# S4D convolution and 16-head attention on one core: set 0 of the seeds last and kept on chip, the first maxima's row ahead of the late stores, eleven products a job

## The chip, the cores and the metric

The kernel runs on one core of a Trainium2 chip. The time is the device's, in microseconds, of one execution; a kernel is judged by the median of several. An execution's profile gives the span from its first to its last instruction, and what each engine did in it: PE (TensorE: products; its weight loads are listed apart as PEld), DVE (VectorE), ACT (ScalarE), POOL (GpSimd) and SP, which here only issues DMA transfers. PE reads its operands from SBUF, the on-chip memory, and writes to PSUM, a second memory of eight banks, from which DVE and ACT evict results.

## The reference

Two independent halves are put side by side in the last axis (896 columns).

```python
# A: a diagonal state-space convolution; L = 2048, D = 448 channels, N = 256 states
dt = exp(log_dt);  A = -exp(log_A_real) + 1j*A_imag;  C = (C_real + 1j*C_imag) * dt[:, None]
K = 2 * einsum("dn,dnl->dl", C, exp((A*dt[:, None])[:, :, None] * arange(L))).real
a = irfft(rfft(u^T, 2L) * rfft(K, 2L))[:, :, :L]^T + u * D_skip
# B: full attention; S = 2048, 16 heads of 28 columns
q, k, v = split(x @ wqkv)
b = (softmax(q k^T * 28**-0.5) v) @ wo
out = concatenate([a, b], -1)
```

All is float32.

## The kernel before

**Seeds.** The convolution's kernel K is built for 56 blocks of eight channels. A block starts from its seeds: low powers of exp(A dt) (the `e` part, 256 columns), of the C-weighted ones (`g`), and factors (`zz`) with which POOL and DVE later double the powers up. Seeds are made in eight sets of seven blocks (`seeds(o)`, `BO = 7`). A set goes through stages: load the parameters into `nat`, scale them (ACT), transpose them on PE (`turn`, into the PSUM tile `pn`), sizes, sines and cosines (`tri`, ACT and DVE), then the tables: `e` into a tile taken from the ring of three `qhat` tiles, `g` and `zz` into an `sg` tile (two of them). POOL clears two columns of the `e` tile first (`places`, a memset). `put_e` and `put_g` store both to DRAM (`sd_d`).

**Projections.** In the same stage x (four chunks of 512 rows) is turned on PE and split into a high part `xh` and a rest `xl`, and the weights likewise, since a float32 product is made of three products in a shorter format: high by high, low by high, high by low. Of the 448 inner rows 112 are taken at a time (`CK`, `NCK`), so that a job, 512 columns of q or k for a group of four heads, or 128 rows of v, takes 4 x 3 = 12 products into one PSUM tile `pm`. There are 48 jobs. ACT and DVE split the result again into `hl` (for the last chunk's q a tile `xn`), and SP stores it to DRAM; q, k and v come back in the layout that attention wants (`qhat`, `khat`, `v`; `load_q`, `load_k`, `load_v`). `kdif` holds differences of k, from which the maxima are made with fewer reductions.

The code of this stage is written in slots, one stage of seeds against a share of the jobs. A scheduler then sets the order on each engine; from `nc.kept = KEPT["a"]` on, the program order is kept.

**Maxima.** Attention goes through 16 units: four groups of heads by four chunks of queries. Softmax needs, for each query, a bound on its scores; four products for each of 16 tiles of queries give it (`max_mm`, `max_pair`; ACT evicts one into `rl`, DVE adds and reduces). For the first unit this is a stage of its own. `max_end` turns the result and makes the row `mh` of it on DVE, and `max_put` sends that row by DMA into `qhat`, so that the score product subtracts it. The second unit's first three tiles (`LEAD = 3`, twelve products) come next; then the steps begin.

**Steps.** Each of 256 steps (16 units by 16 tiles of keys) has four score products `pss`, four exponentials `p` on ACT, eight products with v into `po`, four products `pm` for the maxima LEAD + 16 steps ahead, and between them slots for the convolution: powers of the seeds on POOL (`e_power`) and DVE (`g_powers`), blocks, transforms of u, spectra and outputs. `ORDER` sets the order in a step. Seeds are loaded as `sdb`, three blocks ahead. The next group's keys are loaded while the second unit of a group runs.

What the DMA queues do is set by program order too: SP issues one transfer after another, and a transfer whose wait isn't over holds the rest. In the profile nearly all instructions carry L75, the line of the recording helper; so groups are told apart by tiles.

Of the kernel before, what the change touches and what calls it, by code (L numbers as in the profile page):

```python
# [8 lines left out]
F32 = mybir.dt.float32  # L9
# [18 lines left out]
CK = 112  # L28
NCK = D // CK
# [12 lines left out]
SGB, XB, XL = 2, 5, 4  # L42
# [10 lines left out]
NO = 8  # L53
BO = NB // NO
# [36 lines left out]
def body(ctx, tc, a, out):  # L91
# [50 lines left out]

    kt_g, kd_g, q_u, m_u, mh_u, o_u, rl_u = {}, {}, {}, {}, {}, {}, {}
# [82 lines left out]
    with ExitStack() as st:  # L226
        sst, xst, wst = ExitStack(), ExitStack(), ExitStack()
        t_p = pool(sst, "t_p")
# [19 lines left out]
        def load_nat(o, queue=nc.sync):  # L248
            nats[o] = s_p.tile([PO, 4, 256], F32, name="nat", bufs=2)
# [5 lines left out]
        small = s_p.tile([128, BO, SDF - F_G], F32, name="sg", bufs=SGB)  # L255
# [6 lines left out]
        load_nat(0, nc.scalar)  # L262
# [34 lines left out]
        w_g = k0_t[:CK].rearrange("p g (i s k h e) -> p i s k g h e", i=2, s=2, k=NCK, h=HG)  # L297
        vh = y_p.tile([CK, NCK, D], F32R, name="vh")
        vl = y_p.tile([CK, NCK, D], F32R, name="vl")
        nc.gpsimd.memset(k0_t[:CK].rearrange("p g (n e) -> p (g n) e", e=32)[:, :, DH:].bitcast(F32), 0.0)  # L300
# [5 lines left out]
        for i in range(2):  # L306
            wn = t_p.tile([128, 3, LV, BO * 16], F32, name="tri", bufs=2).rearrange("p t k h -> p (t k h)")
            wn = wn[:CK, :2 * 3 * D].rearrange("p (k s d) -> p k s d", k=2, s=3)
# [22 lines left out]
        def seeds(o):  # L331
# [53 lines left out]
            def places():  # L385
                se = q_p.tile([128, HG, CQ], F32R, name="qhat", bufs=3).bitcast(F32).rearrange("p h q -> p (h q)")
                q["se"] = se = se[:, :BO * F_G].rearrange("p (b f) -> p b f", f=F_G)
                q["sg"] = sg = s_p.tile([128, BO, SDF - F_G], F32, name="sg", bufs=SGB)
                q["e8"] = se.rearrange("p b (c h e) -> p b c h e", c=2, e=8)
                q["g4"] = sg[:, :, :F_Z - F_G].rearrange("p b (c h e) -> p b c h e", c=2, e=4)  # L390
# [73 lines left out]
        def transposes(c):  # L464
            for k in range(NCK):
                pt = ps_t.tile([128, CQ], F32, name="pt")[:CK]
# [3 lines left out]
                xl[k] = x_p.tile([CK, CQ], F32R, name="xl", bufs=XL)  # L470
                nc.scalar.activation(xh[k], pt, AF.Copy)
                nc.vector.tensor_tensor(xl[k], pt, xh[k].bitcast(F32), ALU.subtract)

        def qk_proj(c, s, g):
            pp = w_tile()
            n = 0
            for k in range(NCK):
                for i, x_ in ((0, xh), (1, xh), (0, xl)):
                    nc.tensor.matmul(pp, w_g[:, i, s, k, g].rearrange("p h e -> p (h e)"), x_[k],
                                     start=n == 0, stop=n == 3 * NCK - 1)  # L480
# [28 lines left out]
        def v_proj(c, t):  # L509
# [3 lines left out]
            for k in range(NCK):  # L513
                for w_, x_ in ((vh, xh), (vl, xh), (vh, xl)):
                    nc.tensor.matmul(pp[:, :D], x_[k][:, ts], w_[:, k, :], start=n == 0, stop=n == 3 * NCK - 1)
# [17 lines left out]
        stages = [seeds(o) for o in range(NO)]  # L533
# [27 lines left out]
        for t in range(n_stage):  # L561
# [4 lines left out]
            if t + 1 == PW:  # L566
# [21 lines left out]
        max_end(0, ps_t.tile([128, CQ], F32, name="pt"))  # L588
        max_put(0, nc.scalar)
# [12 lines left out]
    k_pools = [k0_p, kq_p]  # L602
# [52 lines left out]
    def load_sd(b, queue=nc.sync):  # L655
        sds[b] = g_p.tile([128, SDF], F32, name="sdb", bufs=4)
        queue.dma_start(sds[b], sd_d[b // BO][b % BO])

    def k_seeds(b):

        if b not in es:
            es[b] = e = g_p.tile([128, 2, 16, N2], F32, name="e", bufs=2)
            nc.scalar.activation(e[:, :, :, :8], sds[b][:, :F_G].rearrange("p (c h e) -> p c h e", c=2, e=8), AF.Copy)
        else:
            g = g_p.tile([128, 2, 16, N1], F32, name="g", bufs=2)
            nc.scalar.activation(g[:, :, :, :4], sds[b][:, F_G:F_Z].rearrange("p (c h e) -> p c h e", c=2, e=4), AF.Copy)
            egs[b] = es.pop(b), g

    def k_start(b):
        zgs[b] = ps_g.tile([128, CQ], F32, name="zg")  # L670
        nc.scalar.activation(zgs[b][:, :Z_G], sds[b][:, SDF - Z_G:], AF.Copy)

    def e_power(b, i, q):

        t, m = egs[b][0], 8 << i
        zz = sds[b][:, F_Z:].rearrange("p (k f h) -> p k f h", k=6, f=3)
# [368 lines left out]
    for s in range(NS):  # L1045
# [20 lines left out]
        if kt % 4 == 1 and u % NQ == 1 and u // NQ + 1 < G:  # L1066
            load_k(u // NQ + 1, kt // 4, k_pools[(u // NQ + 1) % 2])
# [4 lines left out]
        for op in ORDER:  # L1072
# [96 lines left out]
```

## Time and profile before

| | |
|---|---|
| median of 3 runs | 1276.75 us (1276.06 to 1277.42) |
| the profiled execution | 1278.37 us, span 1276.6 us |
| mean granted TensorE clock | 0.985 |
| PE busy | 1223.9 us, 96% of the span |
| ACT, DVE, POOL busy | 967.5, 923.0, 846.2 us |
| DMA | 205.36 MB, 161 GB/s on average |
| chain that ended last | PE 75%, DVE 8%, POOL 6%, ACT 4%, DMA 3% |

A row of the timeline has the start, the duration, the engine, the operation, output tile <- input tiles, the shape, and in brackets how long the engine was idle ahead of it and what ended that. A group of instructions has its count, then busy time and the mean of one in ns, then idle time. SPq and ACTq are transfers being issued, not engines at work. A piece of the chain has start, duration and what it was.

### The profile page before, as it was taken

How to read it: one execution, taken by the hardware profiler on the slowest of the kernel's cores; microseconds unless marked ns; L12 is line 12 of the kernel's file. 1: busy time of each engine (PE TensorE's matmuls, PEld its weight loads, DVE VectorE, ACT ScalarE, POOL GpSimd, SP SyncE). 2: the span in 40 equal slices, each digit the busy share in tenths (PEclk: the TensorE clock that was granted, in tenths of full speed). 3: DMA queues.
4: the chain of work that ended last, by engine and by line, in shares of the span. 5: the costliest groups of instructions: out<-in, count | busy, mean ns of one | idle time of the engine just before them, and what ended most of it. 6: DMA issues, size and time to landing. Idle time of an engine off the chain costs nothing.

```text
span 1276.6 us, 33328 instructions
## 1 busy us (share of the span) xinstructions
PE 1223.9 (96%) x12641; PEld 699.3 (55%) x12641; DVE 923.0 (72%) x2106; ACT 967.5 (76%) x2162; POOL 846.2 (66%) x728
## 2 busy tenths in 40 slices
PE   7789887999999999999999999999999999999997
PEld 5667664555555555555555555555555545544433
DVE  6788866877777877877788888888897645645111
ACT  6878765788888888888878888888887666656452
POOL 2666750897788888878599999989995222324321
PEclk9889999899999999999999999999999999999999
DMA  7768699446564645375633133422324533657666
GB/s 216 244 223 288 233 304 346 113 93 186 160 149 113 168 119 168 113 235 167 176 94 104 49 88 97 154 81 71 88 54 156 179 131 135 204 170 228 198 170 167
DMA packets 200089, 205.36 MB, mean 161 GB/s; under 512 B 95992, under 2 KB 158520, under 8 KB 197880
## 3 DMA queue, kind: packets, MB, share of 16 engines
q1 hardware_dynamic: 199400, 202.63, 52.6%
q8 instruction: 100, 1.64, 0.5%
q10 hardware_dynamic: 528, 0.59, 0.2%
q14 instruction: 61, 0.50, 0.1%
HBM read 120.73 MB, written 82.18 MB: 159 GB/s over the span
## 4 chain that ended last, share of the span: by engine, by line
PE 75%; DVE 8%; POOL 6%; ACT 4%; issue 3%; DMA 3%; SPq 0%; ACTq 0%; POOLq 0%; DVEq 0%
PE pm L75 43%; PE pss L75 16%; PE po L75 16%; POOL e L75 2%; DVE tri L75 1%; ACT rl L75 1%; POOL qhat L75 1%; DVE mx L75 1%; DVE sg L75 1%; POOL eu L75 1%; ACT tri L75 1%; DVE px L75 1%; DVE qhat L75 1%; DVE hl L75 1%; DMA sd<-qhat 1%
## 5 line engine op out<-in xcount | busy, mean ns | idle before, releaser
L75 ACT ACTIVATE p<-pss 128x512 f32<-128x512 f32 x1024 | 561.0, 610 | 112.5 <-PE pss L75 107.2
L75 PE MATMUL pss<-qhat,khat 128*128 128x512 f32 x1024 | 403.2, 400 | 1.5 <-ACT p L75 1.4
L75 DVE TENSOR_REDUCE mx<-pm 128x1 f32<-128x512 f32 x480 | 308.6, 684 | 109.1 <-PE pm L75 107.2
L75 PE MATMUL pm<-khat,qhat 128*128 128x512 f32 x749 | 325.9, 438 | 6.4 <-ACT rl L75 4.2
L75 POOL TENSOR_TENSOR e<-e,sdb 128x256 f32<-128x256 f32 x168 | 201.8, 1201 | 110.6 <-ACT e L75 101.2
L75 PE MATMUL po<-p,v 128*32 128x512 f32 x2048 | 269.1, 594 | 0.0
L75 POOL TENSOR_TENSOR e<-e,eu 128x256 f32<-128x256 f32 x168 | 248.2, 1477 | 13.2
L75 PEld LDWEIGHTS pm<-khat,qhat 128*128 128x128 f32 x749 | 141.0, 189 | 201.9 <-ACT p L75 47.8
L75 DVE CUSTOM_DVE_ANT_0 rl<-pm,rl 128x512 f32<-128x512 f32 x259 | 178.3, 689 | 72.1 <-ACT rl L75 69.1
L75 PEld LDWEIGHTS pss<-qhat,khat 128*128 128x128 f32 x1024 | 190.6, 189 | 46.7 <-issue 10.8
L75 POOL TENSOR_TENSOR eu<-e,sdb 128x256 f32<-128x256 f32 x168 | 201.9, 1202 | 0.0
L75 POOL TENSOR_TENSOR p<-pr,pr 64x448 f32<-64x448 f32 x64 | 73.2, 1144 | 158.2 <-PE pm L75 132.8
L75 ACT ACTIVATE rl<-pm 128x512 f32<-128x512 f32 x259 | 156.6, 606 | 14.0 <-PE pm L75 8.4
L75 DVE TENSOR_TENSOR g<-g,zg 128x128 f32<-128x128 f32 x392 | 162.2, 414 | 3.4
L75 PE MATMUL pm<-kdif,qhat 128*128 128x512 f32 x249 | 100.5, 403 | 4.3 <-DVE xn L75 2.4
L75 PE MATMUL pm<-xh,khat 112*128 112x512 f32 x256 | 87.3, 425 | 4.9 <-DVE hl L75 1.8
L75 DVE TENSOR_TENSOR zg<-g,zg 128x128 f32<-128x128 f32 x224 | 88.0, 393 | 5.1
L75 PEld LDWEIGHTS pm<-e,g 128*32 128x32 f32 x3584 | 57.2, 109 | 43.4 <-issue 17.1
L75 DVE TENSOR_TENSOR pr<-pm,ub 128x448 f32<-128x448 f32 x64 | 37.0, 620 | 56.4 <-PE pm L75 42.0
L75 PE MATMUL pm<-e,g 128*32 128x64 f32 x3584 | 73.0, 222 | 1.8 <-POOL e L75 1.8
L75 ACT ACTIVATE y<-pm 128x448 f32<-128x448 f32 x48 | 26.5, 553 | 58.2 <-PE pm L75 36.2
L75 ACT ACTIVATE ub<-pm 128x224 f32<-128x224 f32 (+1 forms) x96 | 38.8, 449 | 39.7 <-PE pm L75 37.3
(134 smaller groups left out, 1461.8 us busy)
## 6 DMA issues: line engine op xcount, KB each, us to landing
sdb<-sd SPq DMA_DIRECT2D x55, 336.0 KB
qhat<-q SPq DMA_DIRECT2D x64, 256.0 KB
khat<-k SPq DMA_DIRECT2D x64, 256.0 KB
sd<-sg SPq DMA_DIRECT2D x8, 1456.0 KB
k<-hl SPq DMA_DIRECT2D x16, 512.0 KB
mw<-in_mw SPq DMA_DIRECT2D x16, 512.0 KB
sd<-qhat SPq DMA_DIRECT2D x8, 896.0 KB
yu_d<-ub SPq DMA_DIRECT2D x64, 112.0 KB
```

Source lines behind the costliest of these rows:

```text
L75: i = f(*args, **kw)
```

## The change

- The inner 448 rows are taken as 3 x 128 + 64 (`CK = 128`, `TL = 64`). The last 64 are laid twice into one tile of 128 partitions: x is loaded with its last 64 columns twice (a second, small transfer beside each x load), and after the turn the upper half of `xh` is overwritten with the rest, x minus its high part. The weights' last 64 rows are loaded twice as well. One product then gives high by high and high by low at once, a second the low weights by both: 2 products for this chunk, 3 x 3 + 2 = 11 a job.
- `nat` (two buffers), `sg` (two) and set 0's `e` now lie in one tile in the place of the second group's keys (a pool `k1_p` of its own, open from the start), instead of tiles of their own.
- Sets are made in the order 1 to 7, then 0. Set 0 isn't stored and loaded: its seven blocks are read where they were made. The second group's keys go into the same place, so they are loaded eight steps later (`KL = 8`).
- Of the set before (7), both stores are kept back (`kept`). Before, the two of the seventh set stood between the loads of v and q, and the last set's went in their turn, among the loads of keys.
- After the maxima, SP sends the row right behind the loads of q for two units and the first part of v; the other parts of v and the kept stores come after it. Before, ACT sent it, and then the first seeds.
- The second unit's lead stands right behind, in tiles of the whole stage's PSUM pools (`late_w`) and no longer in three of the next stage's.
- The first step has an order of its own (`ORDER_0`): scores first.

The diff, cut to its core:

```diff
-CK = 112
-NCK = D // CK
+CK = 128
+NCK = 4
+TL = D - 3 * CK
...
+ORDER_0 = ('s0', 's1', 's2', 'k', 's3', 'm0', 'm1', 'v', 'f', 'f', 'v', 'm2', 'm3', 'v')
+KL = 8
-SGB, XB, XL = 2, 5, 4
+XB, XL = 5, 3
+SETS = (1, 2, 3, 4, 5, 6, 7, 0)
...
+        k1_f = k1_p.tile([128, HG * L], F32, name="khat")
+        n_g, n_n = BO * (SDF - F_G), 4 * 256
+        sg_at = (0, HG * L - n_g)
+        sg_view = lambda i: k1_f[:, sg_at[i % 2]:sg_at[i % 2] + n_g].rearrange("p (b f) -> p b f", b=BO)
+        nat_view = lambda i: k1_f[:PO, n_g + i % 2 * n_n:n_g + (i % 2 + 1) * n_n].rearrange("p (a n) -> p a n", a=4)
+        se_view = k1_f[:, n_g:n_g + BO * F_G].rearrange("p (b f) -> p b f", b=BO)
...
-                xns[c, h] = y_p.tile([128, 2, CQ], F32, name="xn", bufs=3)[:, :, :D]
-                nc.sync.dma_start(xns[c, h], xs[:, 2 * h:2 * h + 2, :])
+                xns[c, h] = y_p.tile([128, 2, CQ], F32, name="xn", bufs=3)
+                for d, n, at in ((0, D, 0), (D - TL, TL, D)):
+                    nc.sync.dma_start(xns[c, h][:, :, at:at + n], xs[:, 2 * h:2 * h + 2, d:d + n])
...
-            nc.sync.dma_start(wns[k], wqkv[k * CK:(k + 1) * CK, :].rearrange("p (s d) -> p s d", s=3))
+            for p in range(1 if k < NCK - 1 else 2):
+                n = CK if k < NCK - 1 else TL
+                nc.sync.dma_start(wns[k][p * TL:p * TL + n], wqkv[k * CK:k * CK + n, :].rearrange("p (s d) -> p s d", s=3))
...
-                xl[k] = x_p.tile([CK, CQ], F32R, name="xl", bufs=XL)
                 nc.scalar.activation(xh[k], pt, AF.Copy)
-                nc.vector.tensor_tensor(xl[k], pt, xh[k].bitcast(F32), ALU.subtract)
+                if k < NCK - 1:
+                    xl[k] = x_p.tile([CK, CQ], F32R, name="xl", bufs=XL)
+                    nc.vector.tensor_tensor(xl[k], pt, xh[k].bitcast(F32), ALU.subtract)
+                else:
+                    nc.vector.tensor_tensor(xh[k][TL:], pt[TL:], xh[k][TL:].bitcast(F32), ALU.subtract)
...
-                for i, x_ in ((0, xh), (1, xh), (0, xl)):
+                for i, x_ in ((0, xh), (1, xh), (0, xl))[:3 if k < NCK - 1 else 2]:
...
-        kept_g, kept_e = (stages[NO - 2][i] for i in (-2, -1))
-        stages[NO - 2][-2:] = []
+        kept = stages[-2][-2:]
+        stages[-2][-2:] = stages[-1][-2:] = []
...
-                kept_e.pop()()
                 load_q(1)
-                for c in range(1, NQ):
-                    load_v(0, c)
-                kept_g.pop()()
...
         max_join(0, 2)
-        max_end(0, ps_t.tile([128, CQ], F32, name="pt"))
-        max_put(0, nc.scalar)
+        p_t, p_n, p_x = (lambda p=p, n=n: p.tile([128, CQ], F32, name=n) for p, n in ((ps_t, "pt"), (ps_n, "pn"), (ps_x, "px")))
+        max_end(0, p_t())
+        max_put(0)
+        for c in range(1, NQ):
+            load_v(0, c)
+        for f, in kept:
+            f()
+        late_w = [w_tile] * 3 + [p_t, p_n, p_n, p_x, p_t, p_n, p_n, p_x, p_t]
+        for i in range(LEAD):
+            for kc in range(4):
+                max_mm(1, i, kc, late_w[4 * i + kc])
         sst.close()
...
-    k_pools = [k0_p, kq_p]
+    k_pools = [k0_p, k1_p]
...
+    for b in range(BO):
+        sds[b] = se_view[:, b], sg_view(1)[:, b]
...
-    for b in range(3):
-        load_sd(b, nc.sync if b else nc.scalar)
-    for i in range(LEAD):
-        for kc in range(4):
-            max_mm(1, i, kc)
...
-        if kt % 4 == 1 and u % NQ == 1 and u // NQ + 1 < G:
-            load_k(u // NQ + 1, kt // 4, k_pools[(u // NQ + 1) % 2])
+        uk, kk = divmod(s - KL, NK)
+        if kk % 4 == 1 and uk >= 0 and uk % NQ == 1 and uk // NQ + 1 < G:
+            load_k(uk // NQ + 1, kk // 4, k_pools[(uk // NQ + 1) % 2])
...
-        for op in ORDER:
+        for op in ORDER if s else ORDER_0:
```

Three places in the built order. First PE behind the first unit's maxima, before; `pt<-ident,m` is the turn of the maxima, the products with kdif and khat are the second unit's lead, `pss` the first step's scores:

```order
L75 MATMUL pt<-ident,m_2286 16x128
L75 MATMUL pm_2326<-kdif_1585,qhat 128x512
L75 MATMUL pm_2330<-khat,qhat 128x512
L75 MATMUL pm_2333<-khat,qhat 128x512
L75 MATMUL pm_2336<-khat,qhat 128x512
L75 MATMUL pm_2339<-kdif_1585,qhat 128x512
L75 MATMUL pm_2343<-khat,qhat 128x512
```

and now:

```order
L79 MATMUL pt<-ident,m_2219 16x128
L79 MATMUL pm_2237<-kdif_1544,qhat 128x512
L79 MATMUL pm_2241<-khat,qhat 128x512
L79 MATMUL pm_2244<-khat,qhat 128x512
L79 MATMUL pt<-khat,qhat 128x512
L79 MATMUL pn<-kdif_1544,qhat 128x512
L79 MATMUL pn<-khat,qhat 128x512
L79 MATMUL px<-khat,qhat 128x512
L79 MATMUL pt<-khat,qhat 128x512
L79 MATMUL pn<-kdif_1544,qhat 128x512
```

The products are the same twelve; from the fourth on they are in other tiles than the three `pm`.

Second, SP's queue from the third part of the first group's keys on, before (`k_57` holds these keys in DRAM, `sd_87` and `sd_88` the last two sets of seeds, `q_1_66` the second unit's q, `v_94` to `v_97` v):

```order
L75 DMA khat<-k_57 32x2048 x4
L75 DMA sd_88<-sg 128x7x416
L75 DMA khat<-k_57 32x2048 x4
L75 DMA q_3_80<-xn 128x2x512
L75 DMA v<-v_94 128x512
L75 DMA sd_87<-qhat 128x7x256
L75 DMA v<-v_95 128x512
L75 DMA v<-v_96 128x512
L75 DMA v<-v_97 128x512
L75 DMA qhat<-q_1_66 32x4x512 x4
L75 DMA sd_87<-sg 128x7x416
L75 DMA sd_88<-qhat 128x7x256
```

and now:

```order
L79 DMA khat<-k_57 32x2048 x8
L79 DMA q_3_80<-xn 128x2x512
L79 DMA v<-v_94 128x512
L79 DMA qhat<-q_1_66 32x4x512 x4
L79 DMA qhat<-mh 1x16x128 x2
L79 DMA v<-v_95 128x512
L79 DMA v<-v_96 128x512
L79 DMA v<-v_97 128x512
L79 DMA sd_88<-khat 128x7x416
L79 DMA sd_88<-qhat 128x7x256
```

No store of seeds stands among the loads of keys any more, and the row `mh` has come over from ACT's queue.

Third, POOL at the second fill of a seed tile in a place that was used before, before (`qhat_706` and `qhat_927` are the second and third set's `e` tiles, `qhat_1324` the fifth's):

```order
L75 TENSOR_TENSOR qhat_706<-qhat_706,x_e_834 128x7x16x3
L75 MEMSET qhat_1324 128x7x16 x2
L75 TENSOR_TENSOR gz_872<-tri_721 128x2x112
L75 TENSOR_TENSOR qhat_927<-tri_721 128x7x16 x2
L75 TENSOR_TENSOR dhl_758<-kb_757,dhl_758 128x256
```

and now (`qhat_1082` is the fourth set's, `qhat_1293` the fifth's):

```order
L79 TENSOR_TENSOR dhl_955<-kb_954,dhl_955 128x256
L79 MEMSET qhat_1293 128x7x16 x2
L79 TENSOR_TENSOR tri_923<-tri_923 128x224
L79 TENSOR_TENSOR qhat_1082<-tri_923 128x7x16 x3
L79 TENSOR_TENSOR qhat_1082<-qhat_1082 128x7x16x3
```

The fill has moved from the end of the second set's work to the middle of the fourth's.

More of the change, by code (lines that the diff above doesn't have):

```diff
@@ L248, in load_nat @@
         def load_nat(o, queue=nc.sync):
-            nats[o] = s_p.tile([PO, 4, 256], F32, name="nat", bufs=2)
+            nats[o] = nat_view(SETS.index(o))
             for i, n in enumerate(("A_log_A_real", "A_A_imag", "A_C_real", "A_C_imag")):
@@ L465, in transposes @@
             for k in range(NCK):
[L466 removed]
+                pt = ps_t.tile([128, CQ], F32, name="pt")
                 for t in range(4):
@@ L532, in body @@
             work += jobs
-        stages = [seeds(o) for o in range(NO)]
+        stages = [seeds(o) for o in SETS]
         n_stage = SP * (NO - 1) + len(stages[0]) - SH
         slots = [[] for _ in range(n_stage)]
-        kept_g, kept_e = (stages[NO - 2][i] for i in (-2, -1))
-        stages[NO - 2][-2:] = []
+        kept = stages[-2][-2:]
+        stages[-2][-2:] = stages[-1][-2:] = []
         for o in range(NO):
@@ L653, in body, with load_sd @@
     sds, egs = {}, {}
-    def load_sd(b, queue=nc.sync):
-        sds[b] = g_p.tile([128, SDF], F32, name="sdb", bufs=4)
-        queue.dma_start(sds[b], sd_d[b // BO][b % BO])
+    def load_sd(b):
+        if b >= BO:
+            t = g_p.tile([128, SDF], F32, name="sdb", bufs=4)
+            sds[b] = t[:, :F_G], t[:, F_G:]
+            nc.sync.dma_start(t, sd_d[b // BO][b % BO])
+    for b in range(BO):
+        sds[b] = se_view[:, b], sg_view(1)[:, b]
     def k_seeds(b):
```

36 lines of the change are left out of this document (21 added, 15 removed).

## The prediction

> **What bounds the kernel now.** I read the five stages first (a table of windows cut at the places the chain and the timeline showed), because the change touches only what comes ahead of the attention steps. The columns are busy time per engine (instructions), the granted TensorE clock, the DMA share and GB/s.
>
> ```profile
> core 0: us, PE busy (x) PEld busy (x) DVE busy (x) ACT busy (x) POOL busy (x), PEclk, DMA share, GB/s
> 0.00:186.77 186.77, 160.65 (x706) 126.62 (x706) 145.89 (x288) 142.74 (x347) 108.68 (x149) 0.94 0.76 248
> 186.77:218.70 31.93, 24.75 (x81) 14.24 (x80) 23.06 (x68) 21.23 (x39) 1.88 (x2) 0.95 0.96 347
> 218.70:228.65 9.95, 7.13 (x15) 3.62 (x15) 5.70 (x14) 2.30 (x5) 1.08 (x2) 0.56 0.90 293
> 228.65:1236.00 1007.35, 997.98 (x11471) 541.65 (x11469) 741.48 (x1720) 786.25 (x1743) 726.71 (x574) 1.00 0.47 136
> 1236.00:1276.60 40.60, 33.43 (x374) 13.16 (x372) 6.90 (x18) 15.03 (x28) 7.84 (x4) 0.98 0.68 188
> ```
>
> From 228.65, where the first score product starts, PE is busy 997.98 of 1007.35 us: that stage is PE's own work, and the built order of PE, DVE and ACT after the first steps is the same in both kernels, apart from the tiles that ACT copies seeds from. So the result is decided by when the first score product starts. Ahead of it lie three stages: projections with seeds (186.77 us; PE 86% busy, DVE 78%, ACT 76%, no one engine full), the first unit's maxima (31.93), and the seam (9.95), in which nobody is busy and PE's clock is 0.56.
>
> For the first stage I read the chain of waits from 20 to 192 us: its shares, and its longest stretch of PE.
>
> ```profile
> by line: PE pm L75 12.3%; DVE tri L75 10.2%; issue 9.5%; POOL qhat L75 8.1%; DVE sg L75 7.0%; ACT tri L75 5.8%; DVE px L75 5.4%; DVE qhat L75 5.4%; DVE hl L75 5.0%; DMA sd<-qhat 4.8%; POOL x_e L75 3.3%; SPq L75 2.2%; DVE xl L75 2.2%; DMA kd
> 168.29 10.25 PE pm L75 x36
> ```
>
> The seeds (tri, sg, px, qhat) hold most of the chain, PE's products 12.3% of it, mainly at its end. That is the reason not to credit every product saved.
>
> **The change, part by part.**
>
> *Eleven products a job.* In the timeline three products follow in 0.70 us (184.43 to 185.13), 0.233 us each; in the groups of the first stage the xl products, of which a quarter goes, number 128 and 64.
>
> ```profile
> 184.43 0.40 PE L75 MATMUL pm<-xl,khat 112*128 112x512 f32 x1
> 184.67 0.62 PE L75 MATMUL pm<-xh,khat 112*128 112x512 f32 x2
> 185.13 0.40 PE L75 MATMUL pm<-xl,khat 112*128 112x512 f32 x1
> L75 PE MATMUL pm<-xl,khat 112*128 112x512 f32 x128 | 53.1, 423 | 0.1
> L75 PE MATMUL pm<-vh,xl 112*128 112x448 f32 x64 | 24.4, 388 | 0.0
> ```
>
> So 32 x 0.233 + 16 x 0.204 (448 of 512 columns) = 10.7 us of PE go. The last eight jobs are a pure PE stretch: 8 x 0.233 = 1.9 us, the lower bound; 10.7 is the upper. PE is the busiest engine but only an eighth of the chain, so I take a quarter of the other 8.8, in all -4.0. The DVE subtraction for the stacked chunk has as many columns as before and costs the same.
>
> *Dearer loads at the start.* The weights grow from 448 to 512 rows, and each of the two first x loads gets a 64 KB twin.
>
> ```profile
> tri<-in_B_wqkv SPq DMA_DIRECT2D x4, 588.0 KB
> 10.00:15.00 5.00, 4.38 (x14) 3.24 (x12) 3.62 (x7) 4.08 (x8) 1.37 (x2) 1.00 1.04 215
> 15.00:20.00 5.00, 5.00 (x22) 3.77 (x21) 2.33 (x10) 3.62 (x8) 2.23 (x2) 1.00 0.97 249
> ```
>
> 64/448 of 4 x 588 KB is 336 KB, with the twins 464 KB; at 215 to 249 GB/s, DMA being full there, 2.0 us. PE is at work in 15 to 20, and three jobs share the wait; between 0 and +2.0 I take +1.0. The six later twins are issued a chunk ahead of use, behind other products: 0. [...]
>
> *Fills of seed tiles.* POOL clears the tile of the set three ahead, and waits until that tile's earlier store has landed; what is queued behind it on POOL is the current set's work, and DVE waits for that.
>
> ```profile
> 67.05 2.10 POOL L75 TENSOR_TENSOR qhat<-qhat,x_e 128x336 f32<-128x336 f32 x1
> 69.18 4.11 DMA sd<-qhat
> 73.40 0.56 POOL L75 MEMSET qhat<- 128x112 f32 x2 [4.25 <-DMA sd<-qhat]
> 75.00:80.00 5.00, 3.88 (x22) 2.58 (x20) 1.89 (x5) 3.56 (x8) 3.35 (x7) 1.00 0.55 194
> ```
>
> The wait is on the chain (4.11 us), and DVE idles 3.1 us right after. In the built order this fill moves some fifteen POOL rows back, behind the whole third set, so that wait is over before it is reached. Bounds -4.25 and 0 (ACT's sines come next and could hold the set as long); I take -2.5, near DVE's idle time. The fill before it moves three rows only and I leave its wait. With set 0 last, one tile fewer is filled and one pair of stores goes: 7 x 128 x 672 x 4 B = 2.4 MB less traffic, hidden either way until the maxima.
>
> *The maxima.* The loads of khat now stand ahead of all late stores. The only break in this stage is here:
>
> ```profile
> 210.54 0.69 DVE L75 CUSTOM_DVE_ANT_0 rl<-pm,rl 128x512 f32<-128x512 f32 x1 [0.34 <-ACT rl L75]
> 211.30 0.50 PE L75 MATMUL pm<-kdif,qhat 128*128 128x512 f32 x1 [1.16 <-DVE mx L75]
> 212.18 0.69 DVE L75 CUSTOM_DVE_ANT_0 rl<-pm,rl 128x512 f32<-128x512 f32 x1 [0.94 <-PE pm L75]
> ```
>
> PE waits for a PSUM tile, not for the load: two kdif products stand one behind the other. They do so in the new order too, so 0.
>
> *The seam.* DVE finishes the row of maxima (mh) at 219.62; call this T.
>
> ```profile
> 219.34 0.28 DVE L75 SCALAR_TENSOR_TENSOR mh<-pt,mh 16x128 fp32r<-16x128 f32 x1
> 219.38 2.01 ACTq L75 DMA_DIRECT2D qhat<-mh  x2
> 221.43 0.60 ACTq L75 DMA_DIRECT2D sdb<-sd  x1
> 222.07 0.60 ACT L75 ACTIVATE rl<-pm 128x512 f32<-128x512 f32 x1 [4.46 <-issue]
> 222.70 0.69 DVE L75 CUSTOM_DVE_ANT_0 rl<-pm,rl 128x512 f32<-128x512 f32 x1 [3.09 <-ACT rl L75]
> 222.72 0.79 PE L75 MATMUL pm<-khat,qhat 128*128 128x512 f32 x1 [2.80 <-ACT rl L75]
> 224.40 0.81 SPq L75 DMA_DIRECT2D sdb<-sd  x2
> 227.92 1.28 DVE L75 TENSOR_REDUCE mx<-pm 128x1 f32<-128x512 f32 x2
> 228.65 0.63 PE L75 MATMUL pss<-qhat,khat 128*128 128x512 f32 x1
> 220.00:225.00 5.00, 2.28 (x4) 1.20 (x5) 1.90 (x4) 1.19 (x2) 0.00 (x0) 0.50 0.86 286
> ```
>
> ACT issues three transfers before it may evict the lead's first product: 2.6 us in which DVE and PE stand, PE with three tiles full. After that the lead crawls through three tiles at half clock, and the first score product comes at T + 9.0, with DVE's last lead reduction ending at 229.20, T + 9.6. Now the transfer is SP's, ACT's first eviction can end at T + 0.4, and DVE's three rounds (0.62 + 1.28 = 1.9 each) end at T + 6.1: 3.5 us earlier. The twelve lead products go round all eight PSUM banks; the last of them waits for DVE's fifth operation, T + 3.6, and the score follows at T + 3.9: 5.1 us earlier, if the row is there. SP's first wait behind the row ended at 224.40, T + 4.8 at most, with more stores ahead of it than now. So between -3.5 (DVE sets the early steps) and -5.1 I take -4.3. The v loads and set 7's stores stand behind the row on SP; v's first part is ahead of it, the others are wanted four steps apart. Seeds of blocks 0 to 6 need no load, so POOL starts early; in the steps POOL is 72% busy and gains nothing.
>
> *In the steps.* Khat of the next group is loaded eight steps later and waits for POOL's last reading of block 6; the maxima that want it are eight steps or more further, and DMA is 47% busy: 0.
>
> Sum: -4.0 + 1.0 - 2.5 - 4.3 = -9.8. The profiled run took 1278.37 us, so 1268.6 by its own time; it was 1.6 above the median of 1276.75, so I forecast 1267.0.
>
> **The rivals.**
>
> The front isn't shortened: the seeds' chain on DVE, POOL and ACT hides products and fill alike. For it speaks PE's 12.3%; against it the PE stretch at the end. Then only the start's +1.0 and the seam's -4.3: 1273.5.
>
> The front is PE's after all (86% busy): 10.7 and 4.25 in full, 1276.75 - 10.7 - 4.25 + 1.0 - 4.3 = 1258.5.
>
> The row doesn't travel under the lead, so that the change doesn't do what it says: SP is late for it, or it lands behind v loads, and the first score stays at T + 9. Against it: fewer stores are ahead. 1267.0 + 4.3 = 1271.3.
>
> Slower: the new order puts three nat loads of the fourth set behind two v stores on SP, where one stood.
>
> ```profile
> 45.12 0.62 SPq L75 DMA_DIRECT2D v<-vst  x1
> 45.79 0.84 SPq L75 DMA_DIRECT2D nat<-in_A_A_imag  x1
> 53.30 0.57 SPq L75 DMA_DIRECT2D v<-vst  x1
> 54.77 0.70 PE L75 MATMUL pn<-ident,nat 56*128 56x56 f32 x8 [2.76 <-ACT nat L75]
> 60.00:65.00 5.00, 4.17 (x12) 3.49 (x13) 5.00 (x12) 3.02 (x7) 3.65 (x4) 0.50 0.98 306
> ```
>
> Were they as late as the second store is here, 7.5 us, PE's in-order turn (which waits for them already) would move as far, and PE would run at 0.50 for three more such windows, 2.5 us each: +15.0 - 9.8 = +5.2, 1282.0. It decides once that delay and its half clock cost more than 9.8. Against it: the second store was late here because a seed store stood ahead of it, which now stands behind. [...]
>
> **How the numbers follow.** Forecast 0.47 (its own range 1263 to 1271: the seam's 3.5 to 5.1, the fill's 0 to 4.25, products 1.9 to 6), front not shortened 0.20, front PE's 0.12, row late 0.09, slower 0.07, mixed 0.05. The range goes from 1257.5, the PE rival, to 1276.0, past the first and third rival. A change under 0.2% (2.5 us) can't be told from none here; only a mix of a late row and an unshortened front (1277.8) falls there: same 0.05, slower 0.07, faster 0.88.
>
> **What would show it.** Right: the first score product near 219; no ACT issue between mh and the lead's first eviction; PE's clock at 1.00 through most of the lead; the second fill of a seed tile without a wait; 48 fewer products. Wrong: a first score product later than T + 6; the last projection product not before 184; new waits of PE for nat or of the score product for mh; a stage of steps longer than 1007 us, which I hold fixed and on which, with its size, the whole forecast hangs.

## The result, and the profile after

| | before | after |
|---|---|---|
| median of 20 runs, taken together | 1278.18 us | 1280.78 us |
| lowest and highest | 1276.06, 1280.87 | 1278.45, 1283.60 |
| profiled execution, span | 1278.37, 1276.6 us | 1279.05, 1277.3 us |
| products on PE | 12641 | 12593 |

The ratio is 1.0021 (95% interval 1.0014 to 1.0027): slower by 2.6 us, where 1267.0 was forecast. (The forecast started from the median of three runs, 1276.75, which lay 1.4 us under the median of twenty; what it forecast for the change is -9.8.) The two profiled executions differ by 0.68 us only, so the places below come from traces and the verdicts from medians. The front is everything up to the last projection product.

The five stages of the changed kernel, cut at the same events as the prediction's table (columns as there; first `kdif` product, turn of the maxima, first score, 1236, end):

```profile
core 0: us, PE busy (x) PEld busy (x) DVE busy (x) ACT busy (x) POOL busy (x), PEclk, DMA share, GB/s
0.00:187.91 187.91, 150.80 (x657) 118.31 (x658) 146.91 (x289) 142.35 (x349) 109.56 (x150) 0.93 0.75 248
187.91:219.80 31.89, 25.12 (x82) 14.14 (x80) 22.10 (x66) 20.82 (x37) 0.00 (x0) 0.95 0.66 244
219.80:224.90 5.10, 4.99 (x13) 2.98 (x14) 4.29 (x11) 2.29 (x5) 0.87 (x2) 0.67 0.32 100
224.90:1236.00 1011.10, 999.22 (x11467) 541.43 (x11468) 742.38 (x1723) 786.39 (x1743) 726.38 (x573) 1.00 0.46 137
1236.00:1277.30 41.30, 34.12 (x382) 13.46 (x374) 6.90 (x18) 15.03 (x28) 8.40 (x4) 0.99 0.68 190
```

In these two executions the first stage didn't shrink by 5.5 us (-4.0 + 1.0 - 2.5), it grew by 1.14 (187.91 against 186.77), although PE is busy 9.85 us less in it. The maxima are as long as before (31.89, 31.93). The seam is 5.10 instead of 9.95. So the first score product does start earlier, at 224.90 instead of 228.65. But the gain doesn't last. From T (mh ready: 219.62 before, 220.70 after) to the first score, and from there to the fourth step's first product with v, from which on both kernels keep one rhythm, it is before:

```profile
219.62:228.65 9.03, 6.23 (x13) 3.07 (x11) 5.15 (x12) 2.30 (x5) 1.08 (x2) 0.52 0.88 281
228.65:242.82 14.17, 14.17 (x100) 7.78 (x102) 12.15 (x29) 12.07 (x26) 13.62 (x13) 0.95 0.37 114
```

and after:

```profile
220.70:224.90 4.20, 4.09 (x11) 2.32 (x10) 3.73 (x9) 2.13 (x5) 0.87 (x2) 0.59 0.39 121
224.90:243.44 18.54, 15.95 (x101) 7.89 (x103) 13.59 (x32) 12.26 (x26) 16.02 (x15) 0.91 0.70 228
```

The lead is 4.83 us shorter, the first four steps are 4.37 longer; 0.46 is left. The timeline of those steps in the changed kernel shows the new waits:

```profile
225.33 1.58 ACT L79 ACTIVATE p<-pss 128x512 f32<-128x512 f32 x3 [1.18 <-PE pss L79]
...
227.47 0.62 ACT L79 ACTIVATE rl<-pm 128x512 f32<-128x512 f32 x1
228.12 0.69 DVE L79 CUSTOM_DVE_ANT_0 rl<-pm,rl 128x512 f32<-128x512 f32 x1 [1.44 <-ACT rl L79]
228.14 0.50 PE L79 MATMUL pm<-khat,qhat 128*128 128x512 f32 x1 [0.97 <-ACT rl L79]
...
230.78 0.50 PE L79 MATMUL pm<-khat,qhat 128*128 128x512 f32 x1 [1.17 <-DVE mx L79]
231.45 1.77 PE L79 MATMUL po<-p,v 128*32 128x512 f32 x8
```

With the four scores ahead, ACT makes all four `p` (three, then the copy `zg`, then one) before it evicts the first maxima tile at 227.47. DVE stands 1.44 us for it, PE then stands for ACT and for DVE, and its eight products with v take 1.77 us (1.10 in the kernel before): the granted clock is 0.56 in them.

In the front, two things stand out. POOL's waits at fills of seed tiles aren't gone:

```profile
58.93 0.50 POOL L79 MEMSET qhat<- 128x112 f32 x2 [1.20 <-DMA sd<-qhat]
98.23 0.52 POOL L79 MEMSET qhat<- 128x112 f32 x2 [2.35 <-DMA sd<-qhat]
114.91 0.57 POOL L79 MEMSET qhat<- 128x112 f32 x2 [6.96 <-DMA sd<-qhat]
```

That is 10.5 us in three waits, where 6.2 in two stood before. The second row is the fill that waited 4.25 us at 73.40. It comes 25 us later now and still waits 2.35, for the store of the second set's `e`; the third row's fill waited for nothing before. POOL's last product for that `e` ends at 66.77 here and at 69.15 before, but SP sent its store at 69.18 before (first fence) and sends it at 92.77 now (second):

```profile
69.18 0.37 SPq L75 DMA_DIRECT2D sd<-qhat  x1
```

```profile
91.84 0.36 SPq L79 DMA_DIRECT2D kd<-dhl  x1
92.30 0.42 SPq L79 DMA_DIRECT2D q<-hl  x1
92.77 0.48 SPq L79 DMA_DIRECT2D sd<-qhat  x1
```

The store stands behind others on SP, among them that of `kd`, for which SP stood 9.0 us until POOL had made `dhl`. And PE, with fewer products, waits for evictions more (for those of `hl` and `vst` 11.4 us in the first 188 us, 7.9 before):

```profile
125.51 0.94 PE L79 MATMUL pm<-xh,khat 128*128 128x512 f32 x2 [2.32 <-DVE hl L79]
```

### The profile page after: what moved, and what is told of

The parts are those of the page before. It is cut to its first block, busy times and chain, and to the rows that moved or that the text cites. A ratio compares the mean times of both kernels' runs of the same rounds, so it can differ in the third digit from the quotient of the medians.

```text
span 1277.3 us, 33236 instructions
## 1 busy us (share of the span) xinstructions
PE 1214.3 (95%) x12593; PEld 690.3 (54%) x12593; DVE 922.6 (72%) x2106; ACT 966.9 (76%) x2162; POOL 845.2 (66%) x728
## 2 busy tenths in 40 slices
DMA packets 199511, 201.39 MB, mean 158 GB/s; under 512 B 98040, under 2 KB 158776, under 8 KB 197304
## 4 chain that ended last, share of the span: by engine, by line
PE 77%; DVE 9%; ACT 5%; POOL 3%; DMA 3%; issue 2%; SPq 1%; ACTq 0%; POOLq 0%; DVEq 0%
PE pm L79 43%; PE pss L79 17%; PE po L79 17%; DVE tri L79 2%; DVE mx L79 1%; ACT tri L79 1%; DVE khat L79 1%; ACT rl L79 1%; SPq L79 1%; ACT p L79 1%; POOL qhat L79 1%; DMA khat<-k 1%; DVE px L79 1%; POOL p L79 1%; DVE hl L79 1%
## 5 line engine op out<-in xcount | busy, mean ns | idle before, releaser
L79 DVE TENSOR_REDUCE mx<-pm 128x1 f32<-128x512 f32 x475 | 305.2, 683 | 111.5 <-PE pm L79 109.5
L79 PE MATMUL pm<-khat,qhat 128*128 128x512 f32 x742 | 321.6, 436 | 5.6 <-DVE mx L79 3.1
L79 POOL TENSOR_TENSOR e<-e,sdb 128x256 f32<-128x256 f32 x147 | 176.6, 1201 | 64.6 <-ACT e L79 56.5
L79 PEld LDWEIGHTS pss<-qhat,khat 128*128 128x128 f32 x1024 | 190.7, 189 | 46.6 <-issue 10.8
L79 POOL TENSOR_TENSOR eu<-e,sdb 128x256 f32<-128x256 f32 x147 | 176.8, 1202 | 0.0
L79 PE MATMUL pm<-xh,khat 128*128 128x512 f32 x256 | 83.1, 418 | 10.1 <-DVE hl L79 6.5
```

What stands on the lines that cost most here:

```text
L79: i = f(*args, **kw)
```

## The experiments

Each time is a median, each ratio is to the kernel before, run beside it on the same chip, with its 95% interval. The kernel before stood between 1278.08 and 1278.28 throughout.

### The first step's order

`own_order`, on the changed kernel:

```diff
-        for op in ORDER if s else ORDER_0:
+        for op in ORDER:
```

> The changed kernel, with the usual step order in the first attention step too (maxima and scores in turn) instead of the order with four scores ahead. Theory A (the lead's gain is given back because four scores stand ahead of the first step's maxima: ACT copies four p tiles before it evicts the first maxima tile, DVE idles 1.44 us, PE then waits for DVE and its clock falls to half): the first two steps shrink by 1.5 to 4 us and the median comes to 1277 to 1279.5. Theory B (what PE, ACT and DVE have to do in the lead and the first steps is conserved, the order doesn't matter): within 0.7 us of the changed kernel's 1280.8.

Measured: 1277.74, ratio 0.9999 (0.9990 to 1.0008), so 3.0 us under the changed kernel. Theory A holds. In its trace T is 223.32 (its front ended later, see the last section), and the way from there to the fourth step is

```profile
223.32:227.60 4.28, 3.56 (x12) 1.93 (x11) 3.74 (x9) 2.20 (x5) 1.22 (x2) 1.00 0.43 126
227.60:242.21 14.61, 14.24 (x101) 6.89 (x103) 13.24 (x32) 12.07 (x26) 14.11 (x12) 1.00 0.88 287
```

The lead is as short as in the changed kernel, and the four steps take 14.61 us instead of 18.54: 18.89 in all against 23.20 before, 4.3 us less. That is the seam's whole forecast. Other traces below agree on the first step's order: with four scores ahead the four steps take 18.54 us in `after_as12` and 17.05 in `p12`, with the usual order 14.59 in `own_as12` and 15.70 in `best11`.

### The seam alone

`seam_own`, on the kernel before; nothing else of the change:

```diff
-                kept_e.pop()()
                 load_q(1)
-                for c in range(1, NQ):
-                    load_v(0, c)
-                kept_g.pop()()
...
-        max_put(0, nc.scalar)
+        max_put(0)
+        for c in range(1, NQ):
+            load_v(0, c)
+        for f, in (kept_g, kept_e):
+            f()
+        ...the lead in late_w, as in the change
```

> The kernel before with the seam alone: the row of maxima on SP's queue, the other v parts and the two kept stores behind it, the second unit's lead in all eight banks while it travels; twelve products, the seed order, and the usual step order as before. Theory A (the seam's gain is real where the first step keeps its order): 3.5 to 5 us faster than the kernel before (ratio 0.9961 to 0.9973). Theory B (work of the lead and the first steps is conserved): within 1 us (ratio 0.999 to 1.001).

Measured: 1279.99, ratio 1.0017 (1.0006 to 1.0027): neither. The lead was short (4.32 us), and then

```profile
226.75 0.42 ACT L75 ACTIVATE e<-sdb 128x256 f32<-128x256 f32 x1 [6.09 <-DMA sdb<-sd]
...
227.91 0.80 PE L75 MATMUL pm<-khat,qhat 128*128 128x512 f32 x1 [3.61 <-ACT rl L75]
```

ACT's first copy of seeds stands ahead of its evictions, and its load now travels behind the row, the parts of v and two stores. `seam_early` loads that block's seeds ahead of the maxima:

```diff
                 load_v(0, 0)
                 load_q(1)
+                sd_0 = pool(k0_st, "sd0_p", side="right").tile([128, SDF], F32, name="sdb")
+                nc.sync.dma_start(sd_0, sd_d[0][0])
```

> The seam alone on the kernel before, with one thing added: the first block's seeds are loaded ahead of the maxima into a tile of their own, so ACT's first copy of seeds no longer waits for a load behind the row. With that load behind the row, ACT stood 6.09 us and the run came out 1.8 us above the kernel before. Theory A' (the seam gives its 4.3 us only where the first seeds are on chip): 1273 to 1275.5 (ratio 0.996 to 0.998). Theory B (the lead's and first steps' work is conserved): 1277.5 to 1280.

Measured: 1274.31, ratio 0.9969 (0.9958 to 0.9981), 4.0 us faster than before. Theory A' holds: the seam gives its gain only where the first seeds are on chip, and having them there is worth 5.7 us (1279.99 to 1274.31) in this place.

### Products and loads

`p12`, on the changed kernel, issues each job's first product twice (each with a start, so the second overwrites the first): twelve products again, all else as changed. `b11` is the other side, the kernel before with the products' part of the diff alone (CK, twins, weights, stacking). `loads12` is `b11` with the first product issued twice.

```diff
             for k in range(NCK):
+                if k == 0:
+                    nc.tensor.matmul(pp, w_g[:, 0, s, k, g].rearrange("p h e -> p (h e)"), xh[k], start=True, stop=True)
                 for i, x_ in ((0, xh), (1, xh), (0, xl))[:3 if k < NCK - 1 else 2]:
...the same in the jobs of v
```

> The changed kernel with 12 products a job again: the first product of each job is issued twice, each with a start of its own, so the result is unchanged; loads and stacking stay. Theory C (the seeds' chain on POOL, DVE and ACT, with its fills, paces the front, and the products lie beside it): no more than 2 us slower, the 1.9 us of the last eight jobs at most, so 1280 to 1283. Theory D (products count, and something else in the change eats their gain): 4 to 10 us slower, 1285 to 1291.

> The kernel before with the eleven products alone: stacked fourth chunk, twin loads, 512 weight rows; seeds, seam and steps as before. Theory C: the front keeps its length but for the first loads, so 0 to +2 us against the kernel before (ratio 1.000 to 1.0015). Theory D: products count, -4 us or more (ratio 0.997 or less).

> The kernel before with the stacked fourth chunk, its 512 weight rows and twin loads, but with twelve products a job (the first issued twice): the loads alone. Eleven products with these loads stood 4.8 us above the kernel before. Theory E (the missing products cost, since PE's gaps grow and its clock halves more often): the loads cost 0 to 2 us (ratio 1.000 to 1.0015). Theory F (the loads and their small pieces are the loss, the products weigh nothing): 4 to 5 us slower (ratio 1.003 to 1.004).

Measured: `p12` 1277.71 (0.9998, 0.9985 to 1.0011), `b11` 1282.97 (1.0043, 1.0031 to 1.0055), `loads12` 1277.03 (0.9989, 0.9979 to 0.9999). Neither theory C nor D had this sign: 48 useless products make the changed kernel 3.1 us faster, and `b11` 5.9 us faster. Theory F falls, since the loads alone, in `loads12`, show no loss. I then held theory E (PE's density keeps its clock up). But the scheduler builds the front's order from its own estimate of durations, and with one product more in each job the order of all five queues comes out otherwise. So the order was tied, by edges that set the order and add no wait:

```diff
+FRONT = {"sync": "0-17 20 19 21 18 22-24 ...", "scalar": ..., "gpsimd": ..., "vector": ..., "tensor": ...}
...
+    for e, t in FRONT.items():
+        (each instruction of the front gets an order edge to the one ahead of it in the list)
     nc.kept = KEPT["a"]
```

`b11_as12` has the instructions of `b11` in the order of `loads12`; `l12_as11` the reverse.

> Eleven products a job, loads as changed, all else as in the kernel before, but with every engine's order of the front tied to the one that the scheduler gave the twelve-product version of the same kernel. The two versions with their own orders stood at 1283.0 (eleven) and 1277.0 (twelve). Theory E (PE's density sets its clock: the missing products themselves cost): the order changes nothing, 1281 to 1284. Theory G (the scheduler, given eleven products, made a worse order of DVE, ACT and POOL for the front; the products weigh little either way): 1275 to 1278.

> The reverse: twelve products a job (the first issued twice), with every engine's order of the front tied to the one that the scheduler gave the eleven-product version. Theory E: as its own order, 1276 to 1278. Theory G: the order carries the loss, 1282 to 1285.

| median us | order made for 11 | order made for 12 |
|---|---|---|
| 11 products | 1282.97 (`b11`) | 1275.06 (`b11_as12`) |
| 12 products | 1286.09 (`l12_as11`) | 1277.03 (`loads12`) |

Ratios of the two tied ones: 0.9971 (0.9960 to 0.9981) and 1.0057 (1.0043 to 1.0070). Theory G holds, the second 1.1 us above its range: down a column, 48 products less save 2.0 and 3.1 us; along a row, the order costs 7.9 and 9.1. Theory E falls: at one order fewer products are never slower. The first stages of `b11` and of `b11_as12`, up to the last projection product:

```profile
0.00:191.22 191.22, 155.90 (x658) 122.60 (x658) 145.56 (x287) 142.43 (x347) 105.86 (x148) 0.91 0.74 243
```

```profile
0.00:183.90 183.90, 149.91 (x658) 118.37 (x658) 148.82 (x288) 141.76 (x347) 107.33 (x149) 0.94 0.77 253
```

The same 658 instructions of PE end 7.3 us earlier, with the clock at 0.94 instead of 0.91. PE's busy time is 6.0 us shorter, so in these two executions most of the difference is PE running at the lower clock, and 1.3 us is its idle time. (That tying costs little in itself shows in `b11_evict` below: `b11`'s own order, tied, but for one eviction, takes 1282.96 against 1282.97.)

`after_as12` does this to the changed kernel itself: eleven products, the four scores ahead, only the front's order taken from `p12`.

> The changed kernel as it is, eleven products and the four scores ahead in the first step, with each engine's order of the front tied to the one that its twelve-product version had (1277.7). Theory G (the order carries the loss, and at one order 48 products less save 2 to 3 us): 1274.5 to 1276. If the order matters only without the changed seeds: 1279 to 1281.

Measured: 1273.04, ratio 0.9963 (0.9953 to 0.9974), 1.5 us under theory G's range. The order made for eleven products costs the changed kernel 7.7 us.

### Fills

`ring4` gives the e seeds of the fourth set in line a place of their own in the v tiles.

```diff
+    v_all = v_p.tile([128, 5, NK // NQ, HG, 32], F32, name="v")
...
+                elif o == SETS[3]:
+                    se = v_all.rearrange("p a t h e -> p (a t h e)")[:, :BO * F_G].rearrange("p (b f) -> p b f", f=F_G)
```

> The changed kernel with a fourth place for the seeds' e tiles: the fourth set in line puts its e seeds into the v tiles, idle until the front's end, so each later fill waits for a store that is a whole set older. Theory C (fills on the chain): POOL's three waits for seed stores (10.5 us in all) nearly go, the last projection product moves from 187.9 to 182 to 186, and the median falls by 2 to 6 us to 1275 to 1279. Theory D (the fills lie beside the products): the waits go, and the median stays within 1 us of 1280.8.

Measured: 1282.32 (1.0035, 1.0022 to 1.0049), and POOL still waits 10.5 us in three fills: with the new place all fills moved up by one set, so the waits stayed. It tells nothing on the waits' worth. `fill_late` ties each fill behind the set's own first POOL product:

```diff
-                pol.memset(q["e8"][:, :, 0, :, 0], 1.0)
+                with tc.issue_after(q["gi"]):
+                    pol.memset(q["e8"][:, :, 0, :, 0], 1.0)
```

> The changed kernel with each fill of a seed tile tied behind the set's own first POOL product, so POOL no longer stands at a fill for an earlier set's store; every other engine keeps its order (in the run with the fourth place the fills had moved forward with it and POOL still waited 10.5 us, so that run told nothing on this). Theory C (these waits pace the front): POOL's waits for seed stores fall from 10.5 us to under 2, and the median drops by 2 to 6 us to 1275 to 1279. Theory E (the front is paced by stretches in which PE's clock is halved, and they come with PE's idle gaps, whoever causes them): the waits fall and the median stays within 1.5 us of 1280.8.

Measured: 1280.13 (1.0015, 1.0006 to 1.0024), 0.65 under the changed kernel, the intervals overlapping, so theory C falls here. All its fills are without a wait; three of them:

```profile
94.70 0.51 POOL L79 MEMSET qhat<- 128x112 f32 x2
116.74 0.52 POOL L79 MEMSET qhat<- 128x112 f32 x2
133.24 0.53 POOL L79 MEMSET qhat<- 128x112 f32 x2
```

So in this order some 10 us of POOL's waits are worth less than one.

### Where in the order

In `b11`, a product's wait of 2.88 us for an eviction at 128 us and the half clock behind it (0.51 from 127.50 to 134.30) stood out, and by the count of products `b11` ended its jobs 16 to 30 between 1.6 and 3.8 us behind `b11_as12`, and its 31st 7.9 us behind (133.4 against 125.5). (The longest wait of PE in `b11`'s front, 5.19 us for `kb` ahead of 95.78, loses nothing against `b11_as12`, which waits 3.19 and 2.25 us at that point: 3.1 us behind at the end of the job ahead of it, 2.5 at the end of its own.) `b11_evict` ties `b11`'s own order, with that eviction's copy on ACT moved ahead of the table load and the first of eleven exponentials, which it stood behind, and its subtraction on DVE ahead of seven seed operations.

> Eleven products on the kernel before (1283.0 with its own order), one eviction moved and nothing else: the pair of ACT's copy and DVE's subtraction that clears the projection tile for which PE waits 2.88 us at 128 us goes ahead of ACT's eleven size exponentials and of seven seed operations on DVE. Theory H (this one place carries most of the order's 8 us: the wait, and the half clock from 127 to 135 us behind it): 3 to 7 us faster, 1276 to 1280. Theory I (the loss is spread over the front's order): 0 to 2 us faster, 1281 to 1283.

Measured: 1282.96 (1.0038, 1.0023 to 1.0053), no change. What `b11` shows here

```profile
128.34 1.22 PE L76 MATMUL pm<-xh,khat 128*128 128x512 f32 x2 [2.88 <-DVE hl L76]
```

is in `b11_evict`

```profile
125.46 0.71 PE L85 MATMUL pm<-xh,khat 128*128 128x512 f32 x2
...
131.46 1.22 PE L85 MATMUL pm<-xh,khat 128*128 128x512 f32 x2 [3.19 <-DVE hl L85]
```

The job starts 2.9 us earlier, and PE waits as long for the next of its three tiles, whose eviction stands behind the same block of seed operations. Theory H falls, and theory I's range has it; the place isn't one instruction. Two more runs, both with eleven products on the kernel before: `peact12` ties PE, ACT and DVE to the order made for twelve, POOL and SP to that made for eleven; `b11_as13` takes the order that comes out for thirteen.

> Eleven products on the kernel before, with the order of TensorE, ACT and DVE from the twelve-product version and that of POOL and SP from the eleven-product version, so with POOL's fills where they stood with a wait for seed stores. Theory J (how evictions and seed operations alternate on ACT and DVE, and jobs on TensorE, carries the 8 us): 1274 to 1277, as with all five queues tied (1275.1). Theory C again (POOL's and SP's order, fills and stores, carry it): 1280 to 1283.

> Eleven products on the kernel before, with the order that the scheduler makes for thirteen products a job (the first issued three times). Theory K (the order made for eleven products is an outlier): 1274 to 1277. Theory L (orders scatter by several us, and each new set of durations draws another): anywhere from 1272 to 1285, above 1278 in about half the cases.

Measured: `peact12` 1279.27 (1.0008, 0.9999 to 1.0017), half way: the order of PE, ACT and DVE, taken first, gives 3.7 us of the 7.9, and that of POOL and SP on top of it 4.2. (The other mixture wasn't run, so the shares may not simply add.) Neither theory had that. POOL waits 10.8 us at fills in `peact12`, and 1.3 in `b11_as12`; that this wait is the 4.2 us isn't shown, since other rows of POOL and SP moved with it, and `fill_late` speaks against it. `b11_as13` 1277.09 (0.9996, 0.9987 to 1.0005): 0.1 above theory K's range and inside theory L's. Three orders of the same instructions give 1275.1, 1277.1 and 1283.0. The order for eleven is the worst of three; whether it is an outlier or a draw from a wide spread, three can't tell.

### Together

`p12_own` is `p12` with the usual order in the first step; `own_as12` is `after_as12` with it. `best12` is `loads12` with the seam and the early seed load; `best11` has its order and eleven products.

> The changed kernel with twelve products a job (the first issued twice) and the usual step order in the first step. Theory E with A: the two gains, 3.1 and 3.0 us, lie in different stages and add to 1274 to 1275.5 (ratio 0.9965 to 0.998). If both were the same gain (one number of half-clock stretches that either edit removes): 1277 to 1278.

> The same as the changed kernel with the tied order, and the usual step order in the first step: 1275.4 (twelve products, usual order) less the 2 to 3 us of 48 products, 1272.4 to 1273.4.

> The seam with the early seed load and usual step order, on the front with twelve products and the changed loads: by addition of their separate times (1277.0 for this front, some 4 us for the seam) 1272.5 to 1274.5, under both kernels; by theory B 1276.5 to 1278.

> The kernel before with eleven products, the seam, the early seed load and the usual step order, the front's order tied to that of its twelve-product version (1274.7): less 2 to 3 us, 1271.7 to 1272.7, under both kernels by some 6 us.

| | median us | ratio to before |
|---|---|---|
| `p12_own` | 1275.36 | 0.9971 (0.9958 to 0.9983) |
| `best12` | 1274.73 | 0.9967 (0.9954 to 0.9979) |
| `best11` | 1270.80 | 0.9941 (0.9929 to 0.9954) |
| `own_as12` | 1270.06 | 0.9938 (0.9923 to 0.9953) |

`p12_own` came out as expected. `best12` is 0.2 us above its range: on the front of `loads12` the seam gave 2.3 us by the medians, not 4.0, though in the traces with eleven products the way from T to the fourth step is some 4 us shorter with it (19.92 in `best11`, 23.83 to 23.95 in `b11_evict`, `peact12` and `b11_as13`). `best11` and `own_as12` are 0.9 and 2.3 us under theirs, since 48 products gave 3.9 and 5.3 where 2 to 3 were taken. As the interval of each ratio is 1.1 to 1.9 us either way, such differences are known to some 2 us. `own_as12` beats both kernels: it is the changed kernel, all its parts in place, with two orders set by hand, and stands 10.7 us under it and 8.0 under the kernel before. Its front:

```profile
0.00:182.58 182.58, 152.77 (x658) 119.92 (x658) 148.67 (x289) 142.02 (x349) 110.08 (x150) 0.93 0.78 255
```

Here the order's gain isn't the clock. The changed kernel's front is 188.07 long with PE busy for 150.96 (first row of the last section), at the same 0.93: PE is busy no shorter, it waits 7.3 us less.

## Why the prediction was wrong, step by step

*Products, -4.0.* As a price at a fixed order the term was about right: 48 products less gave -2.0, -3.1, -3.9 (`best12` to `best11`), -4.7 (`p12` to `after_as12`) and -5.3 (`p12_own` to `own_as12`). But it is not what the change does. The step that failed is that I priced the products in an order that stays. I compared the built orders at the seam and at the fills alone and never asked what shorter jobs do to the order of the rest of the front: +7.7 us. This is the larger half of the miss. Why the order made for eleven products is the worse one stays open: it is no single eviction, and both the clock and PE's waits have a part in it. DVE's subtraction for the stacked chunk cost what the others do, as priced: 0.694 and 0.678 us in the changed kernel.

*The seam, -4.3, and "steps 0".* The seam's size was right, to the tenth in the trace of `own_order` and within 0.3 us in the median of `seam_early`. What failed is the sentence that the result is decided by when the first score product starts, with the step order of the first step priced at nothing. The score started at T + 4.2, 4.8 us sooner after T than in the kernel before, and the order with four scores ahead gave most of it back: by the medians 3.0 us (changed kernel to `own_order`), 3.0 (`after_as12` to `own_as12`) and 2.3 (`p12` to `p12_own`). I had written down that DVE's lead reductions end at T + 6.1 (they end at 226.68, T + 6.0), but not that ACT would be busy with `p` just then.

*Set 0 on chip: "POOL starts early ... gains nothing".* This asked after POOL and left out ACT, which copies the first seeds ahead of its evictions. With the load behind the row the seam loses 1.8 us, with the first block's seeds there early it gains 4.0. The load's new place would have been the thing to cost.

*Fills, -2.5.* This step failed too. The fill moved back on POOL as said, but the store that it waits for moved back on SP, from 69.18 to 92.77, so 2.35 us of its 4.25 stayed, and the next fill got a wait of 6.96. I followed one fill in POOL's order, and neither the store in SP's nor the later fills. And the term itself was too large in this order: all waits gone gave 0.65, not clear of none.

*Start loads, +1.0.* The start shows them: the first projection product begins at 10.99 us in the kernel before and at 12.01 to 12.45 in seven traces with these loads (the changed kernel, `p12`, `after_as12`, `own_as12`, `b11`, `b11_as12`, `b11_evict`). Whether this reaches the end, and how much of it is the changed order of the first rows, isn't shown: `loads12` came out 1.1 us under the kernel before, in an order of its own, and orders alone differ by up to 9 us. Nor does a run separate a cost of the twins' small pieces (98040 packets under 512 B in the changed kernel, 95992 before) from that of the added bytes.

*The rivals.* "The front isn't shortened" is what happened, but not for its reason, that the seeds hide the products; its 1273.5 is by chance near `after_as12`. The row was not late. The slower rival's 1282.0 is near the 1280.78, and its mechanism isn't there: PE's turn waits 2.57 us for the fourth set, against 2.76 before. The half clock that it adds, 2.5 us in each of three stretches, no run shows: from the end of this wait to 70 us the clock is 1.00 (0.66 before).

```profile
55.58 0.64 PE L79 MATMUL pn<-ident,khat 56*128 56x56 f32 x7 [2.57 <-ACT khat L79]
```

*The signs I had named.* A last projection product not before 184 (188.07) and a stage of steps that isn't fixed (the first four 4.37 us longer) both came, and both pointed at the steps that failed. Of the signs of being right, no issue of ACT's stood ahead of the lead's first eviction, and 48 products were gone; but the first score came at 224.90 and not near 219, the second fill waited, and the clock in the lead was 0.59 and not 1.00. With both orders set, the sum is -8.0 against the forecast of -9.8.

## What to carry to other kernels

Where a scheduler writes the order, taking instructions out changes the order of everything near them, and that can weigh more than the instructions: tie the old order first, then measure what the edit is worth, then look for an order. A gain at a mark (the first score) counts only at the next place where both kernels run in one rhythm, so cut the table there. And a long wait on one queue says little on its own: 10 us of POOL's waits were worth 0.65 in one order, and moving one late eviction only handed PE's wait to the next tile.

## What the hardware showed that I hadn't expected

The same front can differ by more than the effects in question. The changed kernel and `own_order` have one order on every queue up to the first step, and their profiled executions end the projections at 188.07 and 192.70:

```profile
0.00:188.07 188.07, 150.96 (x658) 118.31 (x658) 146.91 (x289) 142.35 (x349) 109.56 (x150) 0.93 0.75 247
```

```profile
0.00:192.70 192.70, 154.54 (x658) 121.13 (x658) 148.27 (x289) 142.70 (x349) 108.99 (x150) 0.91 0.74 246
```

The difference goes with the granted clock, 0.93 and 0.91: 3.6 of the 4.6 us are PE's longer busy time on the same instructions. In the changed kernel the wait that ends at 125.51 is followed by a stretch of half clock:

```profile
124.40:126.00 1.60, 0.49 (x2) 0.45 (x3) 1.60 (x5) 1.60 (x12) 1.60 (x2) 0.96 1.05 392
126.00:129.50 3.50, 3.50 (x11) 2.69 (x10) 3.50 (x5) 3.48 (x9) 3.42 (x3) 0.53 1.04 367
129.50:134.00 4.50, 4.50 (x22) 3.85 (x21) 3.61 (x9) 3.78 (x7) 2.92 (x6) 1.00 0.92 334
```

PE is busy for all of 126.00 to 129.50, at 0.53. In `own_order` the same product waits 2.28 us, and the clock stays at 1.00:

```profile
126.73 0.73 PE L79 MATMUL pm<-xh,khat 128*128 128x512 f32 x2 [2.28 <-DVE hl L79]
126.73:130.14 3.41, 2.82 (x11) 1.98 (x11) 3.41 (x5) 3.39 (x12) 3.33 (x3) 1.00 1.02 365
```

So in two executions of one order the clock was 0.53 behind a wait of 2.32 us and 1.00 behind one of 2.28. What decides between the two, no row here shows.

At the seam of the kernel before, the clock was at 0.50 at the start of PE's wait of 2.80 us and stayed there to its end; in the 3.41 us ahead of it, with PE busy for 1.64, it was 1.00. So the length of this wait isn't what brought it down.

```profile
216.55:219.96 3.41, 1.64 (x6) 0.57 (x4) 2.21 (x9) 0.63 (x2) 0.00 (x0) 1.00 1.04 401
219.96:222.72 2.76, 0.00 (x0) 0.00 (x0) 0.02 (x1) 0.60 (x1) 0.00 (x0) 0.50 1.05 365
```
